# An attention layer fused with four experts: an earlier load, fewer transfers, and another order of the first five passes

## The chip, the cores and the metric

The kernel runs on one core of one Trainium2 chip. The metric is the device time of one execution in microseconds (us), input and output in HBM; the median of several executions is compared.

A core has a matrix engine (TensorE, PE in the profile; PEld is its loading of weights), VectorE (DVE), ScalarE (ACT), GpSimd (POOL) and SyncE (SP), which here does nothing but issue DMAs. [...] PSUM is the memory that matmuls write to, SBUF the memory for everything else.

## What is computed

```python
# attention: batch 4, heads 8, seq 768, head_dim 40
for t in range(S):
    y[:, :, t] = einsum('bhd,bhde->bhe', r[t], state)
    Sa = einsum('bhde,bhe->bhd', state, a[t])
    state = state * w[t][:, :, None, :] - einsum('bhd,bhe->bhde', Sa, b[t])
    state = state + einsum('bhd,bhe->bhde', v[t], k[t])
x = y.transpose(0, 2, 1, 3).reshape(B * S, H * D)      # 3072 x 320
# experts: 4, w1 320 x 1024, w2 1024 x 320
p = domain_probs / (domain_probs.sum(-1, keepdims=True) + 1e-09)
for e in range(E):
    h = maximum(x @ w1[e], 0.0)
    out += p[:, e:e + 1] * (h @ w2[e])
```

All of it is fp32. The recurrence is evaluated in chunks of 64 tokens, in which it becomes a handful of matmuls and the solution of a small triangular system.

## The kernel before

**Units and passes.** A unit u is one chunk of 64 tokens of two of the four batches; there are 24. The loop over passes (u = 1 to 23) interleaves four things: the state-dependent steps of unit u, the merge for unit u+1, the preparation within unit u+2, and the loads of unit u+3. Pieces of the experts' work for tokens that are already done are put into the gaps, so that TensorE always has something to do.

**The attention side.** `within` is a generator; each yield is a point at which the pass loop may put other work. It makes, in this order: G, a running product of the decays w, from rawW (a transposing copy, L415, and a scan on VectorE); gp, its reciprocal in token layout (L431); n_tok, k_tok and AT (L468 to 477); their transposes NT and KT by matmul (pNT, pKT); causal scores pc; the products pfe or pf and pe, which give F and ET; and EV, the product of ET with V (pev). `substitute` solves the triangular system of a unit on GpSimd, in a chain of small additions and products named Z (L568 to 585), behind two products named M on VectorE. `merge` has three parts: it turns Z into Qc and QTc on VectorE and copies QTc into QT on GpSimd; pY, a matmul with QTc, is copied to Yq on ScalarE; pQ, a matmul with Yq and Qc, is copied to QT on ScalarE. `step` takes QT to psat, then pxr, then pdy, the new state and Y, and last copies Y into xT, from pass 4 on by twelve DMAs on SyncE that wait for Y.

**The expert side.** x @ w1 is done in up pieces (ph; relu to hs on ScalarE), h @ w2 in down pieces. For a chunk of all four batches, a down is two pieces: D1 (p431, three products) and D2 (p75 and p26, two each, with sums of hs made by VectorE in `add_h`). ph, p431, p75, p26 and po share one PSUM tag, "mm", with three buffers; an up piece takes two, D2 takes two. VectorE empties the down's buffers by adds into osb. For one unit alone (units 0 and 1) a down is one piece, po. An up piece has a part with 64 weight rows (`up_last`) and a part with 128 (`up_main`); `lead()` issues the 64-row part of the next piece on its own if that piece is an up piece, and the piece then does the rest.

**The order.** `mix(n)` issues the next n pieces of the list `todo`; `gap` calls it with a number that depends on the pass. In the first five passes (u < EARLY, "early") TensorE's instructions keep the order in which they are written; from pass 5 on a scheduler may move them. All DMAs named here stand on SyncE's queue, in program order. In the middle of each pass stand the loads of unit u+3:

```python
        if u + 3 < NU:
            go(load_raw(begin(u + 3), "WA"))
            load(units[u + 3], "WBKV")
            later.extend(load_raw(units[u + 3], "VR"))
```

Each raw tensor has one buffer in SBUF; natW and natV have two, the other nat tensors one. `load_piece` loads half of one expert's w1 in three DMAs, into two buffers that take turns. `store` writes a unit's 128 rows of the output as two DMAs, one for each batch.

The early passes end so (the second and third part of merge around the state products prn, which are `s_next`'s first part):

```python
        gap(2)
...
            run(m, 1)
            run(s_next, 1)
            run(m)
            gap(3, 1)
```

Of the kernel before, what the change touches and what calls it, by code (L numbers as in the profile page):

```python
# [15 lines left out]
def kernel(  # L16
# [38 lines left out]
    nc = tc.nc  # L55

    B, H, S, D = r.shape
    E, DM, F = moe_w1.shape
    P = 128
    L = 64  # L60
# [4 lines left out]
    NU = NC * B // 2  # L65
    DT = DM - 2 * P
# [18 lines left out]
    def big(name):  # L85
# [6 lines left out]
        out=ident[:], in_=ident[:], pattern=[[1, P]], compare_op=ALU.is_equal, fill=0.0,  # L92
# [27 lines left out]
    HF, HD = NF // 2, DM // 2  # L120
# [67 lines left out]
    def begin(u):  # L188
        q = Unit()
        q.u, q.c, q.bp = u, u // (B // 2), u % (B // 2)  # L190
        q.b = [2 * q.bp, 2 * q.bp + 1]
        q.start, q.end = q.c == 0, q.c == NC - 1
        q.apart = u >= EARLY + 2
        q.n = {}
        units.append(q)
        return q
# [38 lines left out]
    def go(moves, eng=None):  # L235
        for move in moves:
            move(eng or nc.sync)
# [43 lines left out]
    def load_piece():  # L281

        k = len(pieces)
        e, x = k // 2 % E, k % 2
        if k in in_sums:
            t = sums[in_sums[k]]
        else:
            t = sb.tile([P, PIECE], FP32, name="w1p", tag="w1p", bufs=2)
        q = Piece()
        q.main = t[:, 0:2 * HF * P].rearrange("p (g c) -> p g c", g=2)  # L290
        q.last = t[:, 2 * HF * P:PIECE].rearrange("p (f c) -> p f c", c=P)
        cols = slice(x * HF * P, (x + 1) * HF * P)
        moves = [(q.main, moe_w1[e, 0:2 * P, cols].rearrange("(g p) c -> p g c", p=P))]
        for i in range(2):
            half_cols = slice((2 * x + i) * HF // 2 * P, (2 * x + i + 1) * HF // 2 * P)
            moves.append(
                (q.last[i * DT:(i + 1) * DT], moe_w1[e, 2 * P:DM, half_cols].rearrange("d (f c) -> d f c", c=P))
            )
        for to, src in moves:
            tc.keep_in_program_order(nc.sync.dma_start(out=to, in_=src))  # L300
        pieces.append(q)

    def used(n):

        while len(pieces) < n_pieces:
            k = len(pieces)
            if k in in_sums:
                before = k - 5 if k >= 5 else -1
            else:
                at = [x for x in range(k) if x not in in_sums]  # L310
                before = at[-2] if len(at) > 1 else -1
            if before >= n:
                break
            load_piece()

    def load_w2(e):
        tc.keep_in_program_order(nc.sync.dma_start(out=w2_sb[e][:], in_=moe_w2[e].rearrange("(f p) d -> p f d", p=P)))
# [425 lines left out]
    def up_last(k, xT, n):  # L743

        w1 = pieces[k]
        ph = [ps.tile([P, HF // 2, n], FP32, name="ph", tag="mm", bufs=3) for _ in range(2)]

        for f in range(HF // 2):
            for c in range(2):
                for i in range(2):  # L750
                    matmul(
                        out=ph[i][half(c), f, :], lhsT=w1.last[part(i), f, half(c)],
                        rhs=xT[part(i), 2, :], start=(f == 0), stop=False,
                    )
        return ph

    def up_main(k, xT, n, ph):

        w1 = pieces[k]
        h = sb.tile([P, HF, 2 * P], FP32, name="hs", tag="hs", bufs=3)  # L760
        for i in range(2):
            for f in range(HF // 2):
                for g in range(2):
                    at = i * HF // 2 + f
                    matmul(
                        out=ph[i][:, f, :], lhsT=w1.main[:, g, at * P:(at + 1) * P],
                        rhs=xT[:, g, :], start=False, stop=(g == 1 and f == HF // 2 - 1),
                    )
        for i in range(2):
            nc.scalar.activation(  # L770
                out=h[:, i * HF // 2:(i + 1) * HF // 2, 0:n], in_=ph[i][:], func=ACTF.Relu,
            )
        return h

    def up(k, xT, n):
        return up_main(k, xT, n, up_last(k, xT, n))

    def scale(q, e, minus=False):
        return (minus_gate if minus else gate)[:, q.c, q.bp, e:e + 1]

# [4 lines left out]
        else:  # L785
            nc.vector.scalar_tensor_tensor(out=to, in0=p, scalar=sc, in1=to, op0=ALU.mult, op1=ALU.add)  # L786

    def store(q, osb, cols=slice(0, DM), second=nc.sync):
        for i, eng in enumerate((nc.sync, second)):
            row = q.b[i] * S + q.c * L  # L790
            eng.dma_start(out=out[row:row + L, cols], in_=osb[i * L:(i + 1) * L, cols])

    def outputs():
        return sb.tile([P, DM], FP32, name="osb", tag="osb", bufs=2)
# [1 line left out]
    def mixture_of_unit(q):  # L796

        hs, at = {}, 2 * E * q.u

        def ups(e):  # L800
            hs[e] = [up(at + 2 * e + x, q.xT, P) for x in range(2)]
            used(at + 2 * e + 2)
            if q.u == 0 and e + 2 < E:
                load_w2(e + 2)

        def down(e):
            po = ps.tile([P, DM], FP32, name="po", tag="mm", bufs=3)
            for f in range(NF):
                matmul(
                    out=po[:], lhsT=hs[e][f // HF][:, f % HF, 0:P], rhs=w2_sb[e][:, f, :],  # L810
                    start=(f == 0), stop=(f == NF - 1),
                )
            if e == 0:
                q.osb = outputs()
            add(q.osb[:], po[:], scale(q, e), e == 0)
            if e == E - 1:
                stores.append(lambda: store(q, q.osb))

        todo.append(lambda: ups(0))
        for e in range(E):  # L820
            todo.append(lambda e=e: down(e))
            if e + 1 < E:
                todo.append(lambda e=e: ups(e + 1))

# [121 lines left out]
    def begin_later(n):  # L948
        for move in later[:n]:
            tc.keep_in_program_order(move(nc.sync))  # L950
        del later[:n]
# [12 lines left out]
    def lead():  # L964
        if todo and hasattr(todo[0], "lead"):
            todo[0].lead()

    def run(gen, n=99):
        if gen is None:
            return  # L970
        for _ in range(n):
            if next(gen, gen) is gen:
                break
# [100 lines left out]
    for u in range(1, NU):  # L1074
        in_order[0] = u < EARLY
        q = units[u]
        m = s_next = w = w_next = iter(())
        if u + 1 < NU:
            m, s_next = merge(units[u + 1]), begin_step(u + 1)
            w_next = ws[u + 1]  # L1080
        if u + 2 < NU:
            w = ws[u + 2]

        def gap(n, pieces=None):
            at = 4 * u + n
            run(sum_ops, sums_at.get(at, 0))
            mix((1 if at in sparse else 2) if pieces is None else pieces)

        early = u < EARLY
        if early:  # L1090
            begin_later(len(later))
        run(w_next, 99 if early else 1)
        run(s, 1)
        gap(0)


        if early:
            run(s, 1)
        run(w, 1)
        if not early:  # L1100
            run(w_next)
            run(s)

        if early:
            run(w, 1)
            gap(1)
            run(s)
        if u == 1:
            mixture_of_unit(q)
        elif q.bp:  # L1110
            mixture_of_chunk(units[u - 1:u + 1], chunks_x[q.c])
        if not early:
            begin_later(len(later))
            run(w, 1)
            run(m, 1)
            gap(1)

        if u + 3 < NU:
            go(load_raw(begin(u + 3), "WA"))
            load(units[u + 3], "WBKV")  # L1120
            later.extend(load_raw(units[u + 3], "VR"))
        run(w, 2)

        soon = u in (2, 3, 4)
        if soon:
            run(w, 1)
        if early:
            run(m, 1)
        else:
            run(s_next, 1)  # L1130
            run(m, 1)
        if soon:
            substitute(units[u + 2], nc.gpsimd)
        gap(2)

        if not early:
            run(m, 1)
        if not soon:
            run(w, 1)
        if not early:  # L1140
            lead()
            run(s_next, 1)
        if not soon and u + 2 < NU:
            substitute(units[u + 2], nc.gpsimd)
        if early:
            run(w, 1)
        if u + 3 < NU:
            ws.append(within(units[u + 3]))
            run(ws[u + 3], 1)
        if early:  # L1150
            run(m, 1)
            run(s_next, 1)
            run(m)
            gap(3, 1)
            run(s_next, 1)
            mix(0 if 4 * u + 3 in sparse else 1)
        else:
            gap(3)
        s = s_next
# [31 lines left out]
```

## Time and profile before

| | us |
|---|---|
| median of three executions | 1124.0 (1122.39 to 1124.98) |
| profiled execution | 1122.36, of which span 1120.2 |
| TensorE busy | 1076.8 (96% of the span) |
| VectorE, GpSimd, ScalarE busy | 757.0, 501.9, 353.2 |
| TensorE busy, 0 to 28 and 28 to 56 us | 17.72 and 23.04 of 28 |
| TensorE busy, last 28 us | 24.10 |
| one steady pass (D1 at 712.62 to the same D1 at 755.42) | 42.8 |

The span runs from the first to the last instruction of the profiled execution; 2.2 us of the time lie around it. In a line of the timeline the columns are the start, the length, the engine with its line, the operation, what it writes and reads, and how many instructions are taken together; behind it in brackets is how long the engine stood idle before and what ended the wait. "PEclk" is the clock that TensorE was granted, in tenths of the full one. Line numbers such as L76 can be those of a helper: all matmuls have L76, so they are told apart by what they write.

### The profile page before, as it was taken

The page shows a single profiled execution, that of the slowest core. Times are in us where ns is not written, and L with a number is a line of the kernel's source. Part 1 is how long each engine was busy: PE and PEld are TensorE (multiplying, and loading weights), DVE is VectorE, ACT ScalarE, POOL GpSimd, SP SyncE. Part 2 cuts the span into 40 slices and gives each one's busy share as a digit, 9 for nine tenths or more (in the row PEclk, how much of TensorE's full clock was granted, in tenths as well). Part 3 has the DMA queues.
Part 4 walks back from the last instruction along what each step waited for, and adds up shares of the span by engine and source line. Part 5 has one row for each costly group of instructions (what it writes and reads, how often), then busy time and mean ns, then how long its engine had stood idle before and what let it go on. Part 6 is the DMA issues. An engine that isn't in the chain of part 4 may idle for free.

```text
span 1120.2 us, 38531 instructions
## 1 busy us (share of the span) xinstructions
PE 1076.8 (96%) x16100; PEld 961.0 (86%) x16100; DVE 757.0 (68%) x1553; ACT 353.2 (32%) x956; POOL 501.9 (45%) x1272
## 2 busy tenths in 40 slices
PE   6888899898989999999999999999999999999998
PEld 5777777787978989989999998989989899988887
DVE  8665588886657767767767677677677686543343
ACT  2322444233332332333332432342332333321110
POOL 5004676761625635636536437437346346340000
PEclk8899999999999999999999999999999999999999
DMA  7785536335353454553544543543543542231330
GB/s 116 203 250 139 124 68 152 80 95 121 81 110 93 122 126 97 130 123 82 128 99 101 129 107 86 143 100 88 143 106 87 129 103 64 77 90 60 107 90 12
DMA packets 268869, 122.18 MB, mean 109 GB/s; under 512 B 213737, under 2 KB 242073, under 8 KB 268697
## 3 DMA queue, kind: packets, MB, share of 16 engines
q1 hardware_dynamic: 265416, 119.12, 44.0%
q8 instruction: 127, 2.08, 0.8%
q10 hardware_dynamic: 3280, 0.61, 0.3%
q14 instruction: 46, 0.37, 0.1%
HBM read 111.79 MB, written 3.93 MB: 103 GB/s over the span
## 4 chain that ended last, share of the span: by engine, by line
PE 59%; POOL 12%; DVE 9%; issue 5%; ACT 4%; SPq 2%; DMA 2%; DVEq 0%; POOLq 0%
PE ph L76 26%; PE p L76 20%; POOL Z L585 8%; POOL Z L572 4%; PE psat L76 2%; PE pdy L76 2%; DVE M L547 1%; SPq L223 1%; PE pxr L76 1%; PE po L76 1%; PE pfe L76 1%; PE pQ L76 1%; DVE G L419 1%; ACT Yq L619 1%; PE prn L76 1%
## 5 line engine op out<-in xcount | busy, mean ns | idle before, releaser
L76 PE MATMUL ph<-xT,w1p 128*128 128x256 f32 (+3 forms) x3040 | 446.0, 378 | 7.8 <-issue 7.8
L76 PEld LDWEIGHTS ph<-xT,w1p 64*64 64x64 f32 (+1 forms) x3040 | 338.3, 162 | 76.6 <-issue 33.8
L585 POOL TENSOR_TENSOR Z<-Z 128x31 f32<-128x31 f32 (+7 forms) x704 | 259.1, 368 | 55.2
L880 DVE TENSOR_TENSOR a<-hs 128x512 f32<-128x512 f32 x220 | 152.3, 710 | 105.9 <-ACT hs L770 105.9
L572 POOL TENSOR_TENSOR Z<-M,Z 128x62 f32<-128x62 f32 (+7 forms) x352 | 145.8, 414 | 139.0 <-DVE M L563 113.2
L770 ACT ACTIVATE hs<-ph 128x512 f32<-128x512 f32 (+1 forms) x208 | 115.0, 564 | 214.5 <-PE ph L76 213.4
L76 PE MATMUL p<-sums,a 128*128 128x160 f32 x1056 | 164.8, 299 | 0.0
L76 PEld LDWEIGHTS p<-sums,a 128*128 128x128 f32 x1056 | 152.9, 190 | 2.2
L786 DVE SCALAR_TENSOR_TENSOR osb<-p,gate,osb 128x320 f32<-128x320 f32 (+1 forms) x243 | 108.1, 482 | 60.3 <-PE p L76 56.9
L544 POOL COPY below<-F 32x256 f32<-32x256 f32 x48 | 24.0, 501 | 221.0 <-ACT F L502 219.5
L76 PE MATMUL p<-w,a 128*128 128x160 f32 x704 | 106.2, 301 | 1.3 <-ACT hs L770 0.8
L76 PE MATMUL p<-w,hs 128*128 128x160 f32 x704 | 102.9, 299 | 0.0
L76 PEld LDWEIGHTS p<-w,a 128*128 128x128 f32 x704 | 98.3, 190 | 4.4 <-ACT hs L770 4.4
L76 PEld LDWEIGHTS p<-w,hs 128*128 128x128 f32 x704 | 100.2, 190 | 2.2
L604 POOL COPY QT<-QTc 32x256 f32<-32x256 f32 x96 | 50.3, 524 | 75.2 <-DVE QTc L598 35.1
L547 DVE STREAM_TRANSPOSE M<-blocks 128x1024 f32<-128x1024 f32 x24 | 47.3, 1971 | 39.5 <-ACT blocks L541 39.4
L692 ACT COPY RS<-pxr 64x256 f32<-64x256 f32 x88 | 32.4, 368 | 108.5 <-DVE SX L400 43.3
L529 ACT COPY EV<-pev 64x160 f32<-64x160 f32 x96 | 23.5, 287 | 93.4 <-PE pev L76 93.0
L432 DVE RECIPROCAL gp<-gp 128x320 f32<-128x320 f32 x24 | 51.6, 2151 | 0.7
L596 DVE STREAM_TRANSPOSE Qc<-Z 128x256 f32<-128x256 f32 x24 | 15.0, 627 | 46.4 <-POOL Z L585 46.3
L619 ACT COPY QT<-pQ 32x128 f32<-32x128 f32 x96 | 24.7, 257 | 58.9 <-PE pQ L76 57.2
L651 ACT COPY SN<-prn 128x256 f32<-128x256 f32 x44 | 15.0, 371 | 80.4 <-DVE RH L646 77.6
(147 smaller groups left out, 1371.0 us busy)
## 6 DMA issues: line engine op xcount, KB each, us to landing
w1p<-in_moe_w_dram SPq DMA_DIRECT2D x95, 512.0 KB
w1p<-in_moe_w_dram SPq DMA_DIRECT2D x190, 64.0 KB
w<-in_moe_w_dram SPq DMA_DIRECT2D x4, 1280.0 KB
sums<-in_moe_w_dram SPq DMA_DIRECT2D x9, 512.0 KB
natW<-in_w_dram SPq DMA_DIRECT2D x48, 80.0 KB
natB<-in_b_dram SPq DMA_DIRECT2D x48, 80.0 KB
natK<-in_k_dram SPq DMA_DIRECT2D x48, 80.0 KB
out_dram<-osb SPq DMA_DIRECT2D x46, 80.0 KB
```

What stands on the lines that cost most here:

```text
L76: return stated(nc.tensor.matmul(**k))
L432: pin(nc.vector.reciprocal(out=gp[:], in_=gp[:]))
L544: tc.keep_in_program_order(nc.gpsimd.tensor_copy(out=q.below[quarter(i)], in_=q.F[quarter(i), :, 0:Q]))
L547: ins = nc.vector.transpose(out=M[:], in_=cols)
L572: ins = eng.tensor_tensor(out=Z[:, 1:3, 0:n, j + 1:Q], in0=M[:, j:j + 2, None, j + 1:Q].to_broadcast([P, 2, n, m]), in1=Z[:, here, 0:n, j: ...
L585: eng.tensor_tensor(out=z[:, 0], in0=z[:, 0], in1=z[:, x], op=ALU.add)
L604: ins = nc.gpsimd.tensor_copy(out=q.QT[quarter(i), :, quarter(i % 2)], in_=QTc[quarter(i)])
L619: nc.scalar.copy(out=of_slot(to[quarter(2 * r)], y), in_=src)
L692: nc.scalar.copy(out=RS[half(s), x ^ s::2], in_=prs[x][half(s)].rearrange("p (j i) t -> p j i t", i=2),)
L770: nc.scalar.activation(out=h[:, i * HF // 2:(i + 1) * HF // 2, 0:n], in_=ph[i][:], func=ACTF.Relu,)
L786: nc.vector.scalar_tensor_tensor(out=to, in0=p, scalar=sc, in1=to, op0=ALU.mult, op1=ALU.add)
L880: nc.vector.tensor_tensor(out=t[:], in0=x, in1=y, op=op)
```

## The change

Six edits. A w1 piece comes in two DMAs rather than three: the two 64 KB parts are one of 128 KB. A unit's store is one DMA rather than two. The single units' up pieces get a `lead` too. The W loads of unit u+3 (four rawW and two natW DMAs) are begun at the head of the pass; A, B, K, V stay in the middle. In early passes, `lead()` is called ahead of the first work of a pass (the rest of `within` of the next unit, E V among it), and again after `substitute`, followed by merge's pY, both ahead of the third gap; merge's pQ then comes directly after that gap. And pass 4 issues two pieces rather than one in its second gap. The number of matmuls is the same.

```diff
@@ -290,13 +290,10 @@
         q.main = t[:, 0:2 * HF * P].rearrange("p (g c) -> p g c", g=2)
         q.last = t[:, 2 * HF * P:PIECE].rearrange("p (f c) -> p f c", c=P)
         cols = slice(x * HF * P, (x + 1) * HF * P)
-        moves = [(q.main, moe_w1[e, 0:2 * P, cols].rearrange("(g p) c -> p g c", p=P))]
-        for i in range(2):
-            half_cols = slice((2 * x + i) * HF // 2 * P, (2 * x + i + 1) * HF // 2 * P)
-            moves.append(
-                (q.last[i * DT:(i + 1) * DT], moe_w1[e, 2 * P:DM, half_cols].rearrange("d (f c) -> d f c", c=P))
-            )
-        for to, src in moves:
+        for to, src in (
+            (q.main, moe_w1[e, 0:2 * P, cols].rearrange("(g p) c -> p g c", p=P)),
+            (t[:, 2 * HF * P:PIECE], moe_w1[e, 2 * P:DM, cols].rearrange("d (i c) -> i d c", i=2)),
+        ):
             tc.keep_in_program_order(nc.sync.dma_start(out=to, in_=src))
         pieces.append(q)
 
@@ -772,9 +769,6 @@
             )
         return h
 
-    def up(k, xT, n):
-        return up_main(k, xT, n, up_last(k, xT, n))
-
     def scale(q, e, minus=False):
         return (minus_gate if minus else gate)[:, q.c, q.bp, e:e + 1]
 
@@ -785,10 +779,9 @@
         else:
             nc.vector.scalar_tensor_tensor(out=to, in0=p, scalar=sc, in1=to, op0=ALU.mult, op1=ALU.add)
 
-    def store(q, osb, cols=slice(0, DM), second=nc.sync):
-        for i, eng in enumerate((nc.sync, second)):
-            row = q.b[i] * S + q.c * L
-            eng.dma_start(out=out[row:row + L, cols], in_=osb[i * L:(i + 1) * L, cols])
+    def store(q, osb, cols=slice(0, DM), eng=nc.sync):
+        rows = out.rearrange("(b s) d -> b s d", b=B)[q.b[0]:q.b[1] + 1, q.c * L:(q.c + 1) * L, cols]
+        eng.dma_start(out=rows, in_=osb[:, cols])
 
     def outputs():
         return sb.tile([P, DM], FP32, name="osb", tag="osb", bufs=2)
@@ -798,10 +791,22 @@
         hs, at = {}, 2 * E * q.u
 
         def ups(e):
-            hs[e] = [up(at + 2 * e + x, q.xT, P) for x in range(2)]
-            used(at + 2 * e + 2)
-            if q.u == 0 and e + 2 < E:
-                load_w2(e + 2)
+            ph = []
+
+            def lead():
+                if not ph:
+                    ph.append(up_last(at + 2 * e, q.xT, P))
+
+            def piece():
+                lead()
+                hs[e] = [up_main(at + 2 * e, q.xT, P, ph[0])]
+                hs[e].append(up_main(at + 2 * e + 1, q.xT, P, up_last(at + 2 * e + 1, q.xT, P)))
+                used(at + 2 * e + 2)
+                if q.u == 0 and e + 2 < E:
+                    load_w2(e + 2)
+
+            piece.lead = lead
+            return piece
 
         def down(e):
             po = ps.tile([P, DM], FP32, name="po", tag="mm", bufs=3)
@@ -816,11 +821,11 @@
             if e == E - 1:
                 stores.append(lambda: store(q, q.osb))
 
-        todo.append(lambda: ups(0))
+        todo.append(ups(0))
         for e in range(E):
             todo.append(lambda e=e: down(e))
             if e + 1 < E:
-                todo.append(lambda e=e: ups(e + 1))
+                todo.append(ups(e + 1))
 
 
 
@@ -1089,6 +1094,11 @@
         early = u < EARLY
         if early:
             begin_later(len(later))
+        if u + 3 < NU:
+            go(load_raw(begin(u + 3), "W"))
+            load(units[u + 3], "W")
+        if early:
+            lead()
         run(w_next, 99 if early else 1)
         run(s, 1)
         gap(0)
@@ -1103,7 +1113,7 @@
 
         if early:
             run(w, 1)
-            gap(1)
+            gap(1, 2 if u == 4 else None)
             run(s)
         if u == 1:
             mixture_of_unit(q)
@@ -1116,8 +1126,8 @@
             gap(1)
 
         if u + 3 < NU:
-            go(load_raw(begin(u + 3), "WA"))
-            load(units[u + 3], "WBKV")
+            go(load_raw(units[u + 3], "A"))
+            load(units[u + 3], "BKV")
             later.extend(load_raw(units[u + 3], "VR"))
         run(w, 2)
 
@@ -1131,6 +1141,9 @@
             run(m, 1)
         if soon:
             substitute(units[u + 2], nc.gpsimd)
+        if early:
+            lead()
+            run(m, 1)
         gap(2)
 
         if not early:
@@ -1148,9 +1161,8 @@
             ws.append(within(units[u + 3]))
             run(ws[u + 3], 1)
         if early:
-            run(m, 1)
+            run(m)
             run(s_next, 1)
-            run(m)
             gap(3, 1)
             run(s_next, 1)
             mix(0 if 4 * u + 3 in sparse else 1)
```

## The prediction

> **What bounds the kernel now.** I read the page first, then the stretches of 28 us, then the list of waits by part of the run, then the timeline where TensorE stood still.
>
> ```profile
> PE 1076.8 (96%) x16100; PEld 961.0 (86%) x16100; DVE 757.0 (68%) x1553; ACT 353.2 (32%) x956; POOL 501.9 (45%) x1272
> PEclk8899999999999999999999999999999999999999
> ```
>
> TensorE is busy for 96% of the span and the others much less, so only two things can move the time: TensorE's idle time, 1120.2 - 1076.8 = 43.4 us, and its clock. The stretches say where that idle time lies (the columns after the stretch: its length, then busy time of PE, weight loads, DVE, ACT, POOL, then granted clock):
>
> ```profile
> 84.00:112.00 28.00, 24.71 (x378) 20.37 (x371) 15.27 (x31) 8.38 (x24) 13.62 (x36) 1.00 0.59 140
> 112.00:140.00 28.00, 24.76 (x573) 21.19 (x572) 14.81 (x32) 13.32 (x40) 18.87 (x53) 1.00 0.55 124
> 252.00:280.00 28.00, 24.99 (x365) 22.36 (x368) 19.08 (x37) 9.20 (x26) 5.43 (x12) 0.94 0.51 120
> 308.00:336.00 28.00, 23.95 (x341) 21.41 (x340) 16.45 (x33) 8.62 (x23) 8.07 (x23) 0.94 0.51 111
> 364.00:1092.00 728.00, 726.62 (x10679) 656.36 (x10674) 487.61 (x989) 227.20 (x602) 325.62 (x825) 1.00 0.42 105
> ```
>
> The reader is to see three regimes. The first four passes lose some 3 us in each 28. Passes 5 to 7 lose 7.84 us in two large holes and a small one, two of them at a clock of 0.94. And from 364 us to 1092 TensorE loses 1.4 us in 728: there is nothing to gain in the steady passes, only to lose.
>
> The holes of passes 5 to 7 have one cause, which the waits (total us, times, longest) and the timeline give:
>
> ```profile
> PE ph L76 <- issue: 7.8, 3, 4.1
> DVE G L241 <- DMA w1p<-in_moe_w_dram: 8.0, 1, 8.0
> DVE G L241 <- DMA rawW<-in_w_dram: 5.4, 1, 5.4
> ```
>
> ```profile
> 249.18 9.80 SPq L736 DMA_DIRECT2D xT<-Y  x12
> 260.77 1.56 SPq L223 DMA_DIRECT2D rawW<-in_w_dram  x3
> ```
>
> SyncE issues twelve xT copies, then a w1 piece, and only then rawW. VectorE, which executes in order, stands before G<-rawW from 258.7 to 264.11. Behind G in its queue are the sums of hs and the adds that empty p75, and p75's PSUM buffer is the one that the next up piece takes: ph stands until 269.49. The same happens at 318.16 (4.05 us) and 363.56 (0.78).
>
> [...] psat's first 29 matmuls take 1.00 us at 270.37 after the hole of 3.01 us, against 0.75 at 707.89. [...] Here issue time is what is in question: 9.80 us for twelve.
>
> **Part 1: W at the pass's head.** The four rawW and two natW DMAs now stand ahead of the twelve xT copies. G's data is then there before VectorE reaches G. This takes away 3.01 + 4.05 + 0.78 = 7.84 us. The two half-clock spells that follow (3.4 us each at half speed, during which some 1.5 us of full-speed work is lost, from psat and ph being longer by about 1.4 to 1.6 us in sum) go too: -3.0. Together -10.9. A, B and K move nowhere and come earlier by W's place only. rawW has one buffer, and the turn that empties it is in the pass before, so SyncE's queue should not stand on it long.
>
> **Part 2: fewer DMAs** (95 fewer for w1, 23 or so fewer stores). Each issue takes about 0.55 us of SyncE. That lies beside TensorE work everywhere from 364 on, where no up piece waits for its weights longer than 0.4 us. Taken as 0; bounds -1 (early, where SyncE is full) and +1 (the last store is one transfer rather than two in parallel).
>
> **Part 3: the early order.** A piece's 64-row part (0.65 of a 2.60 us half in pass 1, 1.2 us in later passes) now stands ahead of pev; another such part and pY stand ahead of gap 2, and pQ directly behind it. Work is equal; only waits change.
> Pass 1: pev waited 2.61 us for ET and 0.65 of it is now filled. But pY is issued at about 115.5 in the old time, while its input QTc is ready at 119.2:
>
> ```profile
> 117.50 0.52 POOL L585 TENSOR_TENSOR Z<-Z 128x8 f32<-128x8 f32 x2
> 118.71 0.45 DVE L598 STREAM_TRANSPOSE QTc<-Qc 128x256 f32<-128x256 f32 x1
> 123.85 0.68 PE L76 MATMUL pQ<-Yq,Qc 64*64 64x64 f32 x16 [1.33 <-ACT Yq L619]
> ```
>
> GpSimd's solve sets that, and it doesn't move. With pev's 0.65 of shift the new wait is about 4.2; the old wait of 1.33 before pQ goes, as does 0.65: +2.2. [...]
> Passes 2 and 3: the same wait, shrinking as TensorE falls back behind GpSimd: +2.4, then +0.65; the waits that lead fills, before pxr (0.43 in each of three passes) and pQ (0.5 and 0.35), give 2.1 back. Sum +0.9.
> Pass 4 gets one piece more (gap(1, 2)). It covers pNT's 2.26 us and pc's 0.91 us. But G and the adds now stand before Qc on VectorE, so pY waits about 3.1 and the next piece about 1.0 for its bank; with the half-clock spell of 209 us sometimes staying: +0.2. Between passes 4 and 5 a bank wait of 0.65.
> Early total: 2.2 + 1.1 + 0.9 + 0.2 + 0.65 = +5.1, each wait estimated from solve ends; bounds 0 and +9.
>
> **Part 4: what the extra piece does to all later passes.** Pieces go U (up, 4.6 us), D1 (3.4), U, D2 (4.5). Before, a pass from 5 on puts them in the gaps as [U D1][U D2][U D1][U D2], and the old lead() between pfe and psat issued a U's 64-row part. One piece taken early turns every later pass into [D1 U][D2 U][D1 U][D2 U]. lead() then finds a down piece, which has no lead, and does nothing. The steady timeline shows what it used to cover:
>
> ```profile
> 705.99 0.62 PE L76 MATMUL pQ<-Yq,Qc 64*64 64x64 f32 x13
> 706.50 0.64 PE L76 MATMUL pfe<-NT,AT 64*64 64x64 f32 x30
> 706.72 1.10 ACT L619 COPY QT<-pQ 32x128 f32<-32x128 f32 x4 [2.67 <-PE pQ L76]
> 706.97 1.21 PE L76 MATMUL ph<-xT,w1p 64*64 64x256 f32 x14
> 707.89 0.75 PE L76 MATMUL psat<-QT,RH 64*64 64x64 f32 x29
> ```
>
> psat needs all four QT copies. pQ and pfe last 1.15 us (705.99 to 707.14), the copies end at 707.82, and ph filled the rest. Afterwards pQ follows directly on a U whose second relu (0.54 us) stands on ScalarE just ahead of the copies. So the copies run from +0.68 to +1.78 after U's end, and psat starts at about +1.8 where pfe ends at +1.15: a new wait of 0.65, up to 0.95 if the relu starts late. I take 0.85, in passes 5 to 21: 17 x 0.85 = +14.5. In exchange p26 no longer follows a U whose relu is late:
>
> ```profile
> PEld p L76 <- ACT hs L770: 4.4, 13, 0.7
> PE p L76 <- ACT hs L770: 0.8, 3, 0.4
> ```
>
> -5.2. Steady total +9.3; bounds -5 (psat's wait hidden) and +11 (0.95), the bank below apart.
> That D2 now runs straight into U is the other risk: U's second bank is p75's, whose last add ends between 0.69 us before and 0.68 after D2's end in this trace. Before, at least 0.9 us of small matmuls lay between. The sums of hs, which delay these adds, come earlier now, so I take 0.
>
> **Sum.** 5.1 - 10.9 + 9.3 = +3.5. From the profiled execution, 1122.36 (span 1120.2 and 2.2 around it): 1125.9. That execution lies 1.6 below the median of the three, 1124.0; from the median, 1127.5. I say 1127.
>
> **Rivals.**
> A, faster: psat's wait in the steady passes is 0.3 or less, because the copies overlap pQ (they start per quarter, not after its end) or other matmuls are late enough. For it: ScalarE is 32% busy. Against: psat's first matmul takes two quarters at once, and starts 0.02 us after the last copy in the trace. At 0.3: 5.1 - 10.9 + 17 x 0.3 - 5.2 = -5.9, 1118; with nothing at all 1113. It decides below 0.52 us a pass, where the sum reaches -2.2. Absorbed early waits lead the same way. I price it at 1117.
> B, slower: D2 into U waits for p75's adds. There are two D2 in a pass; 0.7 us at one of them is 17 x 0.7 = +12: 1139; at both 1151. For it: the old adds ended as late as +0.68, with the VectorE queue mixed with sums of hs. Against: VectorE is only 68% busy.
> C, slower: the change of W does not do what it says, since SyncE stands at the pass's head on rawW's single buffer or VectorE's queue is held by another load (rawA, still at mid-pass). Then 10.9 stay: 1138.
>
> **Numbers.** A measurement of this kernel can't tell less than 0.2%, 2.2 us, from nothing. Forecast (1121 to 1134 around 1127): 0.45, of which 0.05 faster, 0.15 same, 0.25 slower. A 0.22, B 0.22, C 0.11. Faster 0.27, same 0.15, slower 0.58. The range leaves one in ten at each end: 1114 (A with half the early loss gone) to 1143 (B, one bank wait a pass and a larger early loss).
>
> **What would show it.** In the profile after: no hole over 1 us at ph in passes 5 to 7, and G not waiting for rawW there; clock 1.0 in both stretches. A wait of PE at pY in passes 1 to 4, summing to 8 to 11 us, for QTc. A wait at psat for the QT copies, about 0.85 us, 17 times; none at p for hs. A hole at ph behind D2 in every pass would show B; psat without a wait would show A. The forecast is wrong if TensorE's idle time between 364 and 1092 us stays under 5 us or goes beyond 18.

## The result, and the profile after

The changed kernel takes 1233.0 us (median of six, 1222.6 to 1236.1) against 1124.5 for the kernel before (six, 1120.7 to 1129.0): a ratio of 1.095, 95% interval 1.090 to 1.100. The forecast was 1127, range 1114 to 1143. The direction was right; the size was off by a factor of more than thirty.

The profiled execution took 1229.08 us, of which the span is 1226.9. First the page of the changed kernel (busy time of the engines, then TensorE's granted clock):

```profile
PE 1144.4 (93%) x16100; PEld 979.2 (80%) x16100; DVE 747.8 (61%) x1553; ACT 355.2 (29%) x956; POOL 479.5 (39%) x1272
PEclk8898999899999999899999989999999999999998
```

The same 16100 matmuls, but TensorE is idle for 82.5 us (1226.9 - 1144.4) rather than 43.4, and the busy time itself has grown by 68 us. The clock digits show one reason for the longer busy time: spells below 9 now come again and again up to the end. By the clock's records TensorE had half its clock for 82 us of the time up to its last matmul, before for 31, so that the spells account for some 26 of the 68 us (an estimate: half of the difference). Part 4 below has another reason. The stretch of the steady passes, in the table of stretches, columns as before:

```profile
364.00:1092.00 728.00, 690.82 (x9871) 590.49 (x9864) 444.94 (x919) 214.65 (x576) 301.73 (x812) 0.97 0.38 93
```

Before, TensorE stood still here for 1.4 us and did 10679 matmuls; now it stands still for 37 us, beyond the 18 that the prediction had named as a sign of being wrong, and does 9871, at a clock of 0.97 and a DMA share of 0.38 where it was 0.42. Measured from psat to psat, a steady pass was 42.8 to 43.3 us; now it is 46.9 to 51.5. The waits in this stretch (total us, times, longest):

```profile
DVE RT L241 <- DMA rawR<-in_r_dram: 65.2, 12, 8.0
PE pNT L79 <- DVE n_tok L465: 16.5, 7, 3.6
PE ph L76 <- DVE osb L780: 15.7, 13, 2.1
```

The kernel before has none of the three in this stretch. The first stands at the head of the others: RT is the transposed copy of rawR (VT that of rawV), and VectorE stood at it in no steady pass before. The timeline of VectorE in the changed kernel shows what is queued behind it:

```profile
706.18 0.71 DVE L241 STREAM_TRANSPOSE RT<-rawR 128x512 f32<-128x512 f32 x1 [8.01 <-DMA rawR<-in_r_dram]
```

Behind these 8.01 us stand Y, the state, n_tok, Qc, G, the sums of hs and the adds that empty p75. So pNT waits for n_tok, and an up piece for p75's buffer. The question for the experiments is why rawR lands late.

### The profile page after: what moved, and what is told of

Same layout as the page of the kernel before. It is cut to its first block, busy times and chain, and to the rows that moved or that the text cites. A ratio compares the mean times of both kernels' runs of the same rounds, so it can differ in the third digit from the quotient of the medians.

```text
span 1226.9 us, 38430 instructions
## 1 busy us (share of the span) xinstructions
PE 1144.4 (93%) x16100; PEld 979.2 (80%) x16100; DVE 747.8 (61%) x1553; ACT 355.2 (29%) x956; POOL 479.5 (39%) x1272
## 4 chain that ended last, share of the span: by engine, by line
PE 56%; DVE 17%; DMA 10%; issue 3%; SPq 3%; POOL 3%; ACT 0%; DVEq 0%; POOLq 0%
PE ph L76 28%; PE p L76 19%; DMA rawR<-in_r_dram 7%; DVE a L885 2%; PE psat L76 2%; DVE osb L780 2%; POOL Z L582 2%; DVE G L416 1%; PE pxr L76 1%; SPq L223 1%; SPq L297 1%; POOL Z L569 1%; DVE G L241 1%; DMA rawV<-in_v_dram 1%; DVE Y L704 1%
## 5 line engine op out<-in xcount | busy, mean ns | idle before, releaser
L76 PE MATMUL ph<-xT,w1p 128*128 128x256 f32 (+3 forms) x3040 | 457.2, 386 | 22.5 <-DVE osb L780 18.8
L76 PEld LDWEIGHTS ph<-xT,w1p 64*64 64x64 f32 (+1 forms) x3040 | 332.5, 164 | 124.8 <-issue 73.1
L582 POOL TENSOR_TENSOR Z<-Z 128x31 f32<-128x31 f32 (+7 forms) x704 | 247.8, 352 | 55.2
L76 PE MATMUL p<-sums,a 128*128 128x160 f32 x1056 | 170.7, 305 | 0.0
L76 PE MATMUL p<-w,hs 128*128 128x160 f32 x704 | 107.0, 305 | 0.0
L601 POOL COPY QT<-QTc 32x256 f32<-32x256 f32 x96 | 41.6, 433 | 121.9 <-DVE QTc L595 98.4
L538 DVE COPY blocks<-F 32x256 f32<-32x256 f32 x48 | 16.5, 344 | 103.6 <-ACT F L499 103.2
L544 DVE STREAM_TRANSPOSE M<-blocks 128x1024 f32<-128x1024 f32 x24 | 46.9, 1956 | 39.6 <-ACT blocks L538 39.5
L241 DVE STREAM_TRANSPOSE RT<-rawR 128x512 f32<-128x512 f32 x21 | 14.9, 708 | 76.5 <-DMA rawR<-in_r_dram 68.5
L428 DVE TENSOR_TENSOR gp<-pg,natW 128x320 f32<-128x320 f32 x24 | 11.7, 485 | 56.4 <-PE pg L79 56.4
L616 ACT COPY Yq<-pY 32x128 f32<-32x128 f32 x96 | 24.7, 257 | 50.5 <-PE pY L76 49.4
```

What stands on the lines that cost most here:

```text
L76: return stated(nc.tensor.matmul(**k))
L241: return nc.vector.transpose(out=out.rearrange("p n (x two) -> p n two x", two=2), in_=t.rearrange("p n (two e) -> p n two e", two=2)[:, : ...
L544: ins = nc.vector.transpose(out=M[:], in_=cols)
L582: eng.tensor_tensor(out=z[:, 0], in0=z[:, 0], in1=z[:, x], op=ALU.add)
L601: ins = nc.gpsimd.tensor_copy(out=q.QT[quarter(i), :, quarter(i % 2)], in_=QTc[quarter(i)])
L616: nc.scalar.copy(out=of_slot(to[quarter(2 * r)], y), in_=src)
```

## The experiments

Ratios are to the kernel before on the same chip, with 95% intervals. In diffs, "-" is the kernel that the text names as the starting point.

### First round: the extra piece, W, the order of loads

e1, from the changed kernel:

```diff
-            gap(1, 2 if u == 4 else None)
+            gap(1)
```

> The changed kernel with gap(1) in pass 4 as before, all else of the change kept. Theory 'shift' (the extra piece puts the last rawR DMA of each unit behind a w1 piece's load that waits for the end of an up piece; VectorE then stands at RT, and everything in its queue behind RT is late): the steady pass is 42.8 us again, 1112 to 1128 us in all. Theory 'loads' (W at the head or the merged w1 DMAs delay the queue of SyncE): the steady pass stays near 50 us, 1215 us or more.

Measured: 1236.2 us, 1.099 (1.095 to 1.103). The steady order of TensorE is that of the kernel before again, and the passes still take 46 to 53 us. "Shift" is not the whole cause, or not the cause.

e2, from the kernel before:

```diff
-            gap(1)
+            gap(1, 2 if u == 4 else None)
```

> The kernel before with gap(1, 2) in pass 4 and nothing else. Theory 'shift': steady passes of 47 to 51 us, 1205 to 1240 us. Theory 'loads': 1120 to 1135 us (only the psat wait of about 0.75 us a pass added).

Measured: 1171.8 us, 1.043 (1.038 to 1.048), with steady passes of 46.3 us, each the same. Neither theory: the extra piece costs 3.4 us a pass by itself, but VectorE never waits at RT here.

e3, from the changed kernel: W back in the middle of the pass.

```diff
-        if u + 3 < NU:
-            go(load_raw(begin(u + 3), "W"))
-            load(units[u + 3], "W")
...
-            go(load_raw(units[u + 3], "A"))
-            load(units[u + 3], "BKV")
+            go(load_raw(begin(u + 3), "WA"))
+            load(units[u + 3], "WBKV")
```

> The changed kernel with the W loads in the middle of the pass again. Theory 'shift': no change in the steady passes, 1220 to 1245 us. Theory 'loads' by way of W: the steady pass falls to about 43.5 us, 1125 to 1145 us.

Measured: 1227.7 us, 1.091 (1.086 to 1.097). With or without the edit of W the intervals overlap (1.090 to 1.100 for the changed kernel), and the steady passes stay at 47 to 51 us: W's place is not where the loss comes from.

e4, from the changed kernel:

```diff
-            begin_later(3 if n > 1 else 6)
+            begin_later(4 if n > 1 else 8)
```

"Bank", in the expectation as in the prediction, is one PSUM buffer of the tag "mm".

> The changed kernel with four V and R DMAs begun behind each piece rather than three (eight rather than six behind a single one), so that all sixteen are on SyncE's queue ahead of the last w1 piece of the pass. Theory 'shift by way of rawR': VectorE no longer waits at RT (65 us before), TensorE's waits at pNT and most of those at ph for the bank go, 1130 to 1155 us; what stays is psat's wait of some 0.75 us a pass. Rival 'bank' (the direct succession of D2 and the up piece makes ph wait for p75's adds whatever rawR does): RT's wait goes and ph's wait stays at 1 to 2 us a pass, 1180 us or more.

Measured: 1270.4 us, 1.130 (1.126 to 1.134): slower still. Both theories fall. All rawR DMAs now stand on the queue ahead of the pass's last w1 piece, and VectorE waits for them all the same (waits of e4, steady passes):

```profile
DVE RT L241 <- DMA rawR<-in_r_dram: 57.5, 14, 5.5
```

So it isn't the place in the queue that makes rawR late. What e1 and e4 share with the changed kernel, and e2 lacks, are the merged transfers (and the early order and W, which e3 has cleared). In e1's trace the packets of one merged w1 DMA (128 of 1 KB) can be followed one by one: they lie between 719.6 and 722.6 us, 3.0 us. In the kernel before, 100 of the 128 packets of the two small DMAs start between 715.6 and 716.5, and the last at 718.1. Over the steady passes the time from the first packet to the last is 2.7 to 4.1 us in e1 (median 2.9) and 0.8 to 3.8 in the kernel before (median 1.3). The stretches say how many of the 16 DMA engines were at work, on these packets and all others (the last two columns are DMA share and GB/s), first e1, then the kernel before:

```profile
719.60:722.60 3.00, 0.67 (x40) 0.53 (x35) 2.80 (x7) 1.68 (x6) 0.86 (x2) 1.00 0.32 77
```

```profile
715.60:716.50 0.90, 0.90 (x38) 0.73 (x39) 0.41 (x1) 0.00 (x0) 0.67 (x3) 1.00 0.95 281
```

A packet takes the same 46 ns (median) in both. There are simply fewer at a time: 128 x 46 ns over 3.0 us is two at once. The other packets in e1's stretch, which make its share 0.32, belong to other DMAs.

### Second round: merged w1, and what is left without it

e5, from the kernel before, only the merge of the two small w1 DMAs:

```diff
-        for i in range(2):
-            half_cols = slice((2 * x + i) * HF // 2 * P, (2 * x + i + 1) * HF // 2 * P)
-            moves.append(
-                (q.last[i * DT:(i + 1) * DT], moe_w1[e, 2 * P:DM, half_cols].rearrange("d (f c) -> d f c", c=P))
-            )
+            (t[:, 2 * HF * P:PIECE], moe_w1[e, 2 * P:DM, cols].rearrange("d (i c) -> i d c", i=2)),
```

> The kernel before with one thing of the change: the two 64 KB DMAs of a w1 piece as one of 128 KB whose outermost dimension is 2. Theory 'merged w1' (its 128 packets run on few of the DMA engines: 2.8 to 3.0 us from the first packet to the last in the trace of e1, 0.9 to 1.1 us for the two in the kernel before; four loads a pass, and all that stands behind them on the same queue comes later): the steady pass goes from 42.8 to 48 us or more, 1200 to 1240 us. Rival 'stores or W': at most 1130 us.

Measured: 1202.9 us, 1.071 (1.067 to 1.074), passes of 45 to 52 us. Its waits in the steady passes:

```profile
PE ph L76 <- DMA w1p<-in_moe_w_dram: 12.4, 6, 3.4
DVE VT L241 <- DMA rawV<-in_v_dram: 31.8, 6, 9.6
ACT RS L689 <- DVE SX L397: 153.2, 14, 15.6
PE p L76 <- ACT hs L767: 39.8, 13, 6.9
```

w1 is late at TensorE itself, which the kernel before never shows there, and rawV is late at VectorE (7.5 us before). With this order of pieces the late tensor reaches TensorE by another road. SX and RS are copies of pxr, one by VectorE, one by ScalarE: SX stands behind VT on VectorE, ScalarE stands at RS for SX (42.5 us before), the relu stands behind RS, and the down piece waits for hs (0.8 us before).

e6, from the changed kernel: three w1 DMAs again (e5's diff turned round).

> The changed kernel with w1 pieces in three DMAs again, the rest of the change kept (W at the head, merged stores, early order, extra piece). Theory 'merged w1 and shift': as e2, steady pass 46.3 us, 1160 to 1180 us; RT does not wait for rawR. Rival 'stores or W': 1210 us or more.

Measured: 1181.7 us, 1.052 (1.049 to 1.054); passes of 46.3 us as in e2. It is 10 us above e2, more than "as e2" allowed for at its upper end by 2 us.

e7, the same without the extra piece.

> The changed kernel with three w1 DMAs and without the extra piece: what is left is W at the head, merged stores and the early order. If merged w1 and the shift make up the whole loss: steady pass 42.8 us, the early passes about 5 to 12 us later (that is what the changed kernel shows at pass 5) and the holes of passes 5 to 7 gone in part (7.8 us at most): 1118 to 1135 us. If something else in the change costs in steady passes: 1145 us or more.

Measured: 1158.7 us, 1.031 (1.027 to 1.036). Something else does cost: passes of 43 to 45 and of 47 to 50 us take turns. Every second pass is one with stores. The timeline of SyncE, the stretches and the timeline of VectorE of e7 around one of them:

```profile
834.36 2.64 SPq L787 DMA_DIRECT2D out_dram<-osb  x2
837.05 0.51 SPq L223 DMA_DIRECT2D rawR<-in_r_dram  x1
```

```profile
836.00:838.00 2.00, 2.00 (x20) 1.49 (x12) 1.97 (x4) 0.30 (x1) 1.69 (x5) 1.00 0.13 31
```

```profile
843.85 0.71 DVE L241 STREAM_TRANSPOSE RT<-rawR 128x512 f32<-128x512 f32 x1 [4.89 <-DMA rawR<-in_r_dram]
```

Between 836 and 838 us nothing but the two merged stores is moving, and the DMA share is 0.13, which is 2 of 16. Their 256 packets last from 835.6 to 843.2; the same bytes took from 727.1 to 731.1 in four DMAs before, issue gaps included. The rawR DMA behind them lands at 843.7, half a microsecond after the stores' last packet. Its 128 packets show what it waited for: 112 of them start by 838.7, while the stores are still moving, and the other 16 start between 843.2 and 843.3. Sixteen of 128 is 2 of 16 again, the same share as the stores' 0.13.

e8, from e2, tests what the extra piece costs: lead() finds the up piece behind a down piece too.

```diff
-        if todo and hasattr(todo[0], "lead"):
-            todo[0].lead()
+        for piece in todo[:2]:
+            if hasattr(piece, "lead"):
+                piece.lead()
+                break
```

> The kernel before with the extra piece in pass 4 (as e2, 1171.8 us, steady pass 46.3 us) and a lead() that also looks past a down piece, so that the up piece's 64-row part stands between pfe and psat again, ahead of D1. Theory 'row switches' (each change between full 128-row matmuls and those of 64-row tiles costs about 0.23 us, and the shift adds eight a pass) with the psat wait: psat's 0.67 us and two of the switches go, 1.1 us a pass, 1148 to 1158 us. Theory 'psat wait alone': 0.67 us a pass, 1158 to 1163 us. If the buffers make the lead wait: no gain, 1170 us or more.

Measured: 1189.1 us, 1.058 (1.055 to 1.061), worse than e2. The third case came: the early claim on two buffers makes ph itself wait, 2.3 us a pass where e2 has 1.0:

```profile
PE ph L76 <- issue: 12.7, 13, 1.0
```

```profile
PE ph L76 <- issue: 30.4, 13, 2.5
```

(First e2, then e8.) So the time of this run doesn't tell psat's wait from the row switches. Its trace shows psat's wait by itself, though: with the lead back, psat's 64 matmuls of a pass follow each other within 0.96 us, as in the kernel before (0.99), where e2 takes 1.65.

### Third round: stores, W and the early order by themselves

e9, from the kernel before: the one-DMA store, as in the change.

> The kernel before with one thing of the change: a unit's store as one DMA whose outermost dimension is 2 (batch). Theory 'two engines' (in the trace of e7 the two stores' 256 packets take 7.6 us, at a DMA share of 0.13, which is 2 of 16, and the last rawR DMA behind them lands so late that pNT waits 3.2 us every second pass): every second pass 47 to 49 us, 1150 to 1175 us. Rival 'early order or W' as the cause of e7's 48 us passes: 1120 to 1130 us.

Measured: 1161.5 us, 1.036 (1.032 to 1.039), with most second passes between 46 and 52 us and the others at 43 to 46. The merged store also lengthens the end: from the last add to the end of the span 9.2 us pass (1156.1 to 1165.3) where the kernel before has 3.7 (1116.5 to 1120.2).

e10, from the kernel before: only W at the head of the pass (e3's diff turned round).

> The kernel before with one thing of the change: W of unit u+3 begun at the head of the pass. The prediction's part 1 (the holes of passes 5 to 7 go, 7.84 us and some 3 us of slow clock): 1110 to 1116 us, steady passes 42.8 us. If W at the head is worth nothing by itself: 1121 to 1127 us.

Measured: 1114.0 us, 0.993 (0.990 to 0.995), 0.7% below the kernel before and the lowest of all. The stretches of e10:

```profile
252.00:280.00 28.00, 28.00 (x488) 25.47 (x488) 24.05 (x48) 10.31 (x30) 7.72 (x20) 1.00 0.48 119
308.00:336.00 28.00, 28.00 (x467) 25.24 (x466) 21.22 (x42) 10.02 (x28) 16.35 (x41) 1.00 0.52 121
```

The holes of 3.01 and 4.05 us and the slow clock behind them are gone. SyncE's timeline shows W ahead of the xT copies, where it stood behind them:

```profile
237.88 1.86 SPq L223 DMA_DIRECT2D rawW<-in_w_dram  x4
239.78 1.31 SPq L202 DMA_DIRECT2D natW<-in_w_dram  x2
...
250.25 8.89 SPq L736 DMA_DIRECT2D xT<-Y  x12
```

Two smaller holes at ph stay, 1.29 us at 354.10 and 0.95 at 398.10. In the steady passes the scheduler puts rawW where it was, behind natB and natK, and the passes take 42.7 to 43.2 us as before.

e11, from e7: two DMAs a store again, so that W at the head and the early order are what is left of the change.

> The changed kernel with three w1 DMAs, two DMAs a store and no extra piece: W at the head and the early order are left. Against e10 it shows what the early order costs. By the positions of psat in e7 (pass 5 reached 7 us later than before, passes 5 to 7 shorter by 11 us): 1116 to 1123 us. If the early order costs nothing: as e10, 1110 to 1116 us.

Measured: 1118.0 us, 0.995 (0.994 to 0.997). The early order costs 4 us against e10 (95% interval 2 to 6). The steady passes are 42.7 to 43.1 us.

### Last: the shape or the count

e12, from the kernel before: the same bytes of w1 in the same number of DMAs, cut by columns instead of by partitions.

```diff
-        for i in range(2):
-            half_cols = slice((2 * x + i) * HF // 2 * P, (2 * x + i + 1) * HF // 2 * P)
-            moves.append(
-                (q.last[i * DT:(i + 1) * DT], moe_w1[e, 2 * P:DM, half_cols].rearrange("d (f c) -> d f c", c=P))
-            )
+        last = moe_w1[e, 2 * P:DM, cols].rearrange("d (i c) -> i d c", i=2)
+        for n in range(2):
+            half_cols = slice(n * HF // 4 * P, (n + 1) * HF // 4 * P)
+            moves.append((t[:, 2 * HF * P:PIECE][:, half_cols], last[:, :, half_cols]))
```

> The kernel before with the two small DMAs of a w1 piece cut the other way: each brings half the columns for all 128 partitions (outermost dimension 2, rows of 512 B), where before each brings all columns for 64 partitions. Bytes and the number of DMAs stay. Theory 'shape' (a DMA whose outermost dimension is 2 runs on two of the 16 engines): as slow as e5 or slower, 1195 us or more, and the 256 packets take 2.5 us or more. Theory 'count' (one DMA in place of two is what loses): 1120 to 1130 us.

Measured: 1198.7 us, 1.066 (1.060 to 1.072); in the steady passes the 256 packets of 512 B take 3.1 to 4.9 us (median 3.3). The shorter rows are not the reason: a packet takes 27 ns (46 with 1 KB), and 256 x 27 ns over 3.3 us is two at once again. Bytes and count are those of the kernel before, and two DMAs with a dimension of 2 outermost are here as slow as the one of e1 (median 2.9 us), where the two with 64 outermost took 1.3. It is the shape.

## Why the prediction was wrong

**The step that failed is part 2**, "Taken as 0; bounds -1 and +1". It counted the issue time of SyncE and took for granted that the same bytes move in the same time. They don't: merged w1 alone costs 79 us (e5), merged stores alone some 39 (e9). What differs is how many packets are under way at once. In the steady passes of the changed kernel the 128 packets of a merged w1 DMA take 2.7 to 4.2 us (59 DMAs, median 3.0), with 2.06 packets under way on average (median); in the kernel before those of the two small DMAs take 0.8 to 3.8 (median 1.3), with 5.2. The 256 packets of two merged stores take 6.7 to 8.0 us with 2.0 to 2.1 under way; in four DMAs before, 3.3 to 4.9 with 4.8 to 7.0. Both merged DMAs have 2 as the outermost dimension on the HBM side: `i d c` for w1, and batch, token, column for the store. In the kernel before it is 64 in both. The experiments agree: share 0.13 with the stores alone under way (e7), and two packets at once for w1's small rows, in one DMA (e1) or in two (e12). Which other outermost dimensions would be slow wasn't measured, nor why 2 is. The diff showed the shape, but no profile of the kernel before could show what it costs, as that kernel has no such DMA.

The loss then travels by the waits that the prediction described for passes 5 to 7, only for another tensor. In e7 the last 16 of a later DMA's 128 packets start only at 843.2, when the stores' last packet is done, 4.5 us after the other 112. VectorE stands at RT meanwhile (4.89 us there, up to 8.01 in the changed kernel) or at VT (up to 9.6 in e5), with n_tok, the state and p75's adds queued behind it: in the changed kernel RT starts at 706.18, the state at 707.46, n_tok at 708.75. That these 16 packets stood on DMA engines which the stores held is a reading; the packets' records name no engine.

**Part 1, W at the head: right.** Forecast -10.9. From psat of pass 5 to psat of pass 8 the kernel before takes 135.8 us, e10 125.3: -10.5. In whole runs it is 0.7%, some 8 us, as two smaller holes appear. In the changed kernel none of it is left: the same stretch is 137.1 us. Rival C named this amount and, as its second reason, another load in VectorE's queue. That is what the trace shows, mainly for a tensor that it did not name: ahead of the hole of 3.04 us at 322.96 VectorE stood 2.79 us at RT for rawR and 1.49 before the copy of rawA, and not at G for rawW. Part 1's two spells of half clock (0.50 in the records) last 3.41 us each, as counted. The length of a hole alone doesn't tell whether one follows. One did behind 3.01 us in the kernel before (half clock from 270.51) and behind 2.14 in the changed one (617.46 to 619.60, half clock from 619.90), or 2.5 from the start of the last matmul to the start of the next; none did behind 2.61 us in the kernel before (94.92 to 97.53).

**Part 3, the early order: right in kind and nearly in size.** Forecast +5.1, of which 0.85 for pass 4 and the step to pass 5 belong to the extra piece, which e11 hasn't got; measured +4.0 (e11 against e10), and psat of pass 5 comes 5.3 us later. The 1.1 in its sum is for the clock in pass 1, an estimate of the author's that no trace of the kernel before shows; in the changed kernel there is a spell of half clock there, 6.83 us from 118.14 on. In the changed kernel the waits at pY appear where they were put (waits from 84 us on), and with 8.5 us for these two lines they lie in the forecast sum of 8 to 11, though 0.6 of it is not for QTc. By pass they are 2.9, 1.2, 0.6 and 3.8 where about 4.2, 2.4, 0.65 and 3.1 were forecast, so that the sum is nearer than its terms:

```profile
PE pY L76 <- DVE QTc L595: 7.9, 3, 3.8
...
PE pY L76 <- DVE G L415: 0.6, 1, 0.6
```

**Part 4, the extra piece: right in direction, too small by six.** Forecast +0.55 us a pass (9.3 in all); measured 3.4 a pass and 48 us in all (e2). The parts, from e2's trace. psat's wait came as worked out: its matmuls take 0.66 us longer than in the kernel before and begin 0.17 later behind pfe, 0.83 in all where 0.85 was taken. Timeline of ScalarE, then of TensorE:

```profile
736.78 0.60 ACT L770 ACTIVATE hs<-ph 128x512 f32<-128x512 f32 x1 [1.13 <-PE ph L76]
737.40 1.10 ACT L619 COPY QT<-pQ 32x128 f32<-32x128 f32 x4
```

```profile
737.18 0.64 PE L76 MATMUL pfe<-NT,AT 64*64 64x64 f32 x30
737.80 0.86 PE L76 MATMUL psat<-QT,RH 64*64 64x64 f32 x6
```

The relu holds ScalarE until 737.4, the four copies end at 738.5, and psat, whose first matmuls are modelled from 737.80, crawls until then. Rival B came too, on top of the forecast rather than in its place: D2 into U, which part 4 took as 0, waits for p75's adds once a pass. From one matmul to the next are 1.36 us, and U's 64-row part takes 2.64 us there against 1.02 in the pass's other three: 1.62 lost. TensorE, then VectorE:

```profile
730.38 0.64 PE L76 MATMUL ph<-xT,w1p 64*64 64x256 f32 x2
732.00 4.74 PE L76 MATMUL ph<-xT,w1p 64*64 64x256 f32 x30 [0.98 <-issue]
```

```profile
730.93 0.68 DVE L880 TENSOR_TENSOR a<-hs 128x512 f32<-128x512 f32 x1
731.53 0.37 DVE L786 SCALAR_TENSOR_TENSOR osb<-p,minus_gate,osb 128x160 f32<-128x160 f32 x1
```

The second p75 add ends at 731.9, held up by a sum of hs; ph goes on at 732.0. The profile names no releaser, but in all 13 passes ph goes on 0.10 us after that add's end. A third part wasn't in the sum at all, the switches between tile shapes (last section), about 0.8 us (an estimate: eight more at 0.1). With p26's wait of 0.24 us gone, this makes 0.83 + 1.62 + 0.8 - 0.24 = 3.0 of the 3.4; the remaining 0.4 isn't assigned. These are parts read from the trace; only psat's was taken away by a run (e8). They also show that busy time can grow without the clock: psat's wait and the switches count as busy, and e2's TensorE is busy for 1120.1 us against 1076.8 at the same mean clock (0.987 and 0.986).

**The rivals, the readings and the range.** One reading was too wide and bears on no sum: the first four passes do not lose some 3 us in each 28, since the stretches from 140 to 196 us lose 1.06 and 0.74. All named rivals looked at waits between engines. None looked at how many packets of a transfer are under way at once, and the range couldn't hold what no case contained.

**What stays open.** The losses overlap: alone they are 79, 39 and 48 us, the early order adds 4, W gives 8 back, and all together make 109. For the stores part of the reason is seen: in e6, with the extra piece, all steady passes take 46.3 us although its stores are merged. e6's 10 us above e2 have two places: its psat of pass 5 comes 5.2 us later, as the early order would have it, and the time from the last add to the end is 9.2 us rather than 3.7, as in e9. In e4 pNT waits for n_tok in 13 steady passes (49.6 us) where the changed kernel has 7 such waits (16.5 us); why there are more wasn't traced.

## What to carry to other kernels

Before merging DMAs to save issue time, write out the outermost dimension on both sides, and measure the merged transfer by itself if the merge changes it. Here it went from 64 to 2 on the HBM side: w1's small rows then took 3.0 us rather than 1.3 (medians), with two packets under way at a time, and behind two such stores the last 16 packets of a rawR DMA came 4.5 us after the others (e7). The idle-free steady state was a finished interlock of order, buffers and landings here; a single extra piece far upstream shifted it for the rest of the run (e2: passes of 46.3 us rather than 42.8), so compare the pattern of the steady pass and not only the place of the edit. And test the edits of a bundle one by one: here the only one found to gain, W at the head, gives 1114.0 us alone and disappears in the sum.

## What the runs showed of the hardware

**Switches of tile shape cost TensorE time here.** From the start of the last matmul of a group to the start of the next group's first, medians in ns over the steady passes of the kernel before and of e2, worked out from the records of the traces:

```
128-row -> 128-row (within p)                  136
128-row p -> 64-row (ph, pe, pQ)               229
64-row -> 64-row, next group (pe -> pxr)        38
64-row -> 128-row (psat, pxr, pY, pdy -> p)    148 to 179
```

Each switch cost about 0.1 us either way here, an estimate from this table: 229 - 136 into 64 rows, 148 - 38 and more out of them. (e8's expectation had 0.23, the whole step.) The kernel before makes 8 a pass, since each small group is followed by an up piece that begins with 64 rows; with the order shifted by one piece there are 16.

**The issues on SyncE took longer too.** The longest issue of a w1 DMA on SyncE (columns min, median, max in ns) rose from 1563 in the kernel before, with a median of 495, to

```profile
L297 SPq DMA_DIRECT2D w1p<-in_moe_w_dram x190: 362/546/3739, 28.0 to 1188.8; - x190
```

in the changed kernel. All issues of SyncE together, summed from the records, are 776 us for 1327 DMAs before and 814 for 1198 now, so that fewer DMAs did not even make the queue shorter. With 1327 again, but w1 cut by columns, they are 939 (e12). That the two packets at a time are the reason isn't shown; the DMAs in question also bring more packets each.
